# A fused attention and gMLP block: V's weight parts reordered, products moved into the first cycle, layer norm's factors moved into the spatial weights, ScalarE's side work limited

## The chip, the cores and the metric

The kernel runs on one core of one Trainium2 chip. A core has a matrix engine (TensorE, in the profile PE, with PEld for its weight loads), a vector engine (VectorE, DVE), an engine for activation functions (ScalarE, ACT), a general engine (GpSimd, POOL) and one that mostly issues DMAs (SyncE, SP). They run side by side, each working through its own list of instructions in order, and wait for each other by semaphores. Matmuls read SBUF and write PSUM.

The metric is the time of one execution on the device in microseconds (us), the median of several. Before the change it is 1957.76 us (1957.56 to 1959.02 in three runs).

## The reference

The input x (2048 x 512, all float32) is layer-normed to xn, and three things are added:

```python
x = A_x
xn = _layernorm(x, axis=-1)
return x + _A_ref(xn, A_wqkv, A_wo) + _B_ref(xn, B_w_in, B_w_sp, B_b_sp, B_w_out)
```

A is attention with 32 heads of 16 columns: qkv = xn @ wqkv, a softmax over 2048 keys of q k / 4, the sum over v, and a product with wo. B is a gated MLP over 1792 columns in two halves:

```python
z = _gelu(jnp.einsum("bsd,df->bsf", x, w_in))
z1 = z[..., :Fh]
z2 = _layernorm(z[..., Fh:], axis=-1)
g = jnp.einsum("ts,bsf->btf", w_sp, z2) + b_sp[None, :, None]
return jnp.einsum("bsf,fd->bsd", z1 * g, w_out)
```

Fh is 896. The spatial weights w_sp (2048 x 2048) mix the rows of z2, so a factor that belongs to row s of z2 may stand on column s of w_sp instead.

## The kernel before

**Products in two parts.** Dense products run in a reduced float32 form (F32R). To keep precision each operand is split into a high part, which is its rounded copy, and a low part, the operand less the high part; `mm3` (L169) adds three matmuls per 128-row block: low-free, low of the one, low of the other (L170, L171, L172 in the profile). What the text calls a product is one such triple over 512 (or 448) columns. A copy on ScalarE or a cast on POOL makes the high part, a subtraction on DVE or POOL the low one.

**Start.** Lines L836 to L906 load x and V's weights, normalise x (`norm_x`: statistics on DVE, the normalisation at L268 on ScalarE), transpose it on PE (`turn_x`), split it (`split`: copy L58 on ScalarE, subtraction L167 on DVE) and make V (`v_tile`) and the first Q and K. V's weights come in four row blocks wv0 to wv3. POOL casts all four (L857), DVE subtracts for blocks 0 to 2 and POOL for block 3 (`end` with `high`, L191).

**Attention.** From L995 a loop runs over half cycles (`half`). A cycle takes three tiles of scores (`scores`, tile st, L955), the exps of them on ScalarE (`exp`, tile pf, 128 x 1024), PV products (`pv`, tile o, L929), and, 27 tiles ahead, three tiles of scores in the other orientation (`max_mm`, tile mx, L650), whose maxima DVE takes (`max_red`, L658). An even half has two exps and one maximum, an odd half one and two. st and mx share three PSUM slots in turn. The halves below zero have mx only.

**Everything else is filler.** The dense products of Q and K (`qk_rest`), of the gMLP's halves (`z2_all`, `z1_all`), the spatial products (`spatial`), the output products (`mlp_out`, `attn_out`) stand in a queue of generators, and at the end of each odd half some are taken by a credit that spreads what is left over the tiles up to number 931. Before tile 0 each half may take four. Their evictions and what follows run on as generators in `side` (L1045): each is advanced once a half, if DVE's own account of the half (`load["D"]`) is under its limit. `bg` holds the loads and preparations of weights (`prepare`, `end`: on POOL a cast L196 and a subtraction L197).

**The planner's clock.** All of this is decided when the program is written out; the order of every engine's list is then fixed. A half counts 2.7 us (`HALF`); `gps(us)` adds a POOL operation's assumed time to POOL's own clock, and `pool_done` or `prepare` let later steps wait until that clock is reached. An `act` is booked as 0.16 + n/1400 us. Where a product's weights aren't ready by that clock, the queue pauses.

**z2.** `z2_norm` (L371) takes one 128-row tile of z2 through the gelu (POOL and one Tanh on ScalarE), the statistics (DVE, L393), the factors (small POOL operations, L396 to L404), the normalisation (Identity on ScalarE, L406), and the split into parts in two pieces of 512 and 384 columns (copy on ScalarE, subtraction on POOL, L412), which go to DRAM. z1's gelu (`z1_gelu`, L453) ends on DVE instead of POOL when POOL's clock is over 4 us behind.

Of the kernel before, what the change touches and what calls it, by code (L numbers as in the profile page):

```python
# [40 lines left out]
def fused_block(ctx, tc, x, wqkv, wo, w_in, w_spT, b_sp, w_out, out):  # L41
# [11 lines left out]

    load = {"A": 0.0, "D": 0.0}

    def act(out, in_, func, n, **kw):
        load["A"] += 0.16 + n / 1400.0
        return nc.scalar.activation(out, in_, func, **kw)  # L58

    def dve(n, rate=1):  # L60
# [12 lines left out]

    mrow = cp.tile([P, 32], F32R, name="mrow")
    nc.vector.memset(mrow.bitcast(F32), 0.0)


    qst = [cp.tile([P, S], F32R, name=f"qst{a}") for a in range(2)]
# [37 lines left out]
    def gps(us):  # L116
        pool[0] = max(pool[0], clock()) + us
        return nc.gpsimd
# [66 lines left out]
        move(dst, src)  # L185
        return t, rw, n

    def end(loaded, low=None, high=False):
        t, rw, n = loaded
        if high:  # L190
            low.tensor_sub(t[:, 1, :n], rw[:, :n], t[:, 0, :n].bitcast(F32))  # L191
        elif low:
            nc.scalar.activation(t[:, 0, :n], rw[:, :n], AF.Copy)
            low.tensor_sub(t[:, 1, :n], rw[:, :n], t[:, 0, :n].bitcast(F32))
        else:
            gps(0.6).tensor_copy(t[:, 0, :n], rw[:, :n])  # L196
            gps(1.3).tensor_sub(t[:, 1, :n], rw[:, :n], t[:, 0, :n].bitcast(F32))  # L197
        return t

    def prepare(out, loads, freed=None):  # L200


        loads, flight, made = list(loads), [], []
        while loads or flight or made:
            if made and clock() >= made[0][0]:
                _, k, t = made.pop(0)
                out[k] = t
            if flight and now[0] >= flight[0][0]:
                _, k, l = flight.pop(0)
                t = end(l)  # L210
                made.append((pool[0], k, t))
                rawfree.append(pool[0])
            if loads and len(rawfree) > 0 and clock() >= rawfree[0] and (freed is None or freed and now[0] >= freed[0]):
                rawfree.pop(0)
                if freed:
                    freed.pop(0)
                k, *a = loads.pop(0)
                flight.append((now[0] + 2, k, begin(*a)))
            yield
# [80 lines left out]

    def qk_group(m, g, w, tags=("d",)):
        for a in range(2):
            if now[0] < -2 and m:
                tags = ("d", "o")
            acc = dpsum(f"qk{m}_{a}_{g}", tags[a % len(tags)], ND)
            for c in range(ND):
                t = xnT[g, c]
                mm3(acc, w[a][:, 0, c * P:(c + 1) * P], w[a][:, 1, c * P:(c + 1) * P], t[:, 0, :], t[:, 1, :], c == 0, c == ND - 1)
                yield 650 + 0.5 * (c == ND - 1)
            if m == 0:  # L310
                run(qk_split(m, g, a, acc))
# [59 lines left out]
    def z2_norm(t, z):  # L371
# [27 lines left out]
        gps(0.3).tensor_mul(rs[:, 2:3], rs[:, 1:2], rs[:, 1:2])  # L399
        gps(0.3).tensor_mul(rs[:, 2:3], rs[:, 2:3], rs[:, 0:1])  # L400
        gps(0.3).tensor_scalar(rs[:, 2:3], rs[:, 2:3], -0.5, 1.5, ALU.mult, ALU.add)
        gps(0.3).tensor_mul(rs[:, 1:2], rs[:, 1:2], rs[:, 2:3])
        gps(0.3).tensor_mul(rs[:, 2:3], mv[:, 0:1], rs[:, 1:2])
        gps(0.3).tensor_scalar(rs[:, 2:3], rs[:, 2:3], -1.0, 0.0, ALU.mult, ALU.add)  # L404
        yield from pool_done()
        act(z, z, AF.Identity, FH, bias=rs[:, 2:3], scale=rs[:, 1:2])  # L406
        for j, (lo, w) in enumerate(((0, 512), (512, 384))):
            yield
            hl = hilo(f"z2hl{t}_{j}")
            act(hl[:, 0, :w], z[:, lo:lo + w], AF.Copy, w)  # L410
            yield
            gps(0.0025 * w).tensor_sub(hl[:, 1, :w], z[:, lo:lo + w], hl[:, 0, :w].bitcast(F32))  # L412
# [422 lines left out]
    with tc.manual_schedule(engines=engines):  # L835
# [17 lines left out]
        run(load_x(2))  # L853
        ones = big.tile([P, 512], F32, tag="raw", name="ones", bufs=3)
        nc.vector.memset(ones[0:32, 0:P], 1.0)
        for t, rw, n in wv:
            nc.gpsimd.tensor_copy(t[:, 0, :], rw)  # L857
        norm = norm_x(0, 2)
        next(norm)
        next(norm)  # L860
        wv = [end(l, (nc.vector, nc.gpsimd)[c == 3], True) for c, l in enumerate(wv)]
        turn_x(0, 0, 2)
        next(norm)
        nc.gpsimd.dma_start(cscr.rearrange("o (a b) -> (o a) b", b=P), ones[0:16, 0:P])
# [130 lines left out]
        for half in range(-2 * LEAD // 3, 2 * (N // 3 + 4)):  # L995
            b = 3 * (half // 2)
            ms = [b + LEAD] if half % 2 == 0 else [b + LEAD + 1, b + LEAD + 2]
            ns = [n for n in ([b, b + 1] if half % 2 == 0 else [b + 2]) if 0 <= n < N]
            now[0] = half
            flush()  # L1000
            for n in ns:
                if n == 16:
# [7 lines left out]
            tiles = [(scores, n) for n in ns]  # L1010
            for i, m in enumerate(ms):
                tiles.insert(1 if half % 2 == 0 else 2 * i, (max_mm, m))
            for make, n in tiles:
                make(n)
            while ended:
# [91 lines left out]
```

## Time and profile before

| what | us |
|---|---|
| median of three runs | 1957.76 |
| profiled execution | 1960.21 |
| its span, first to last instruction | 1958.4 |
| PE busy | 1938.7 |
| DVE busy | 1373.7 |
| ScalarE busy | 1232.5 |
| POOL busy | 725.5 |

The profile is of one execution. Its stages can be told by the tiles that PE writes: the start up to about 85 us, the halves without scores up to 140, then Q and K up to about 230, z2 to 455, z1 to about 675, the spatial products to about 1570, and the outputs. A row of the order of time gives start, duration, engine, line, operation, tiles and shape, and in brackets how long the engine was idle before it and what it waited for. Successive matmuls overlap, so a matmul's time in PE's list is the distance from one start to the next rather than its duration.

### The profile page before, as it was taken

The numbers are of one execution on the slowest core, as the hardware profiler recorded it, in microseconds if no ns is written. First come the engines' busy times: TensorE is split into PE (matmuls) and PEld (weight loads), VectorE is DVE, ScalarE is ACT, GpSimd is POOL, SyncE is SP. The second block draws the span as 40 slices with busy tenths as digits, with TensorE's granted clock in tenths as the row PEclk, the third lists the DMA queues.
The fourth block names the chain that finished last, engine by engine and source line by source line (L and its number), as shares of the span: only waits on it lengthen the run. The fifth ranks groups of instructions, "written<-read, shape, count | busy, mean of one in ns | idle before, by whom it ended". The sixth has DMA issues, their size and how long they took to land.

```text
span 1958.4 us, 32641 instructions
## 1 busy us (share of the span) xinstructions
PE 1938.7 (99%) x12559; PEld 1049.7 (54%) x12559; DVE 1373.7 (70%) x1565; ACT 1232.5 (63%) x1407; POOL 725.5 (37%) x790
## 2 busy tenths in 40 slices
PE   8999999999999999999999999999999999999998
PEld 7765555555555555555555555555555555555543
DVE  5356777777767677777777767777777777777872
ACT  4347778888677666656566656665666655556664
POOL 3334278889776931026122531017112400002100
PEclk9999999999999999999999999999999999999999
DMA  7566344363535535365545745346454645355323
GB/s 260 201 219 183 104 120 117 111 179 107 144 132 153 183 117 141 101 166 156 142 137 162 202 131 134 104 120 205 110 158 144 180 140 137 106 147 160 105 73 113
DMA packets 229202, 284.23 MB, mean 145 GB/s; under 512 B 35176, under 2 KB 134136, under 8 KB 226168
## 3 DMA queue, kind: packets, MB, share of 16 engines
q1 hardware_dynamic: 217240, 272.64, 47.9%
q0 software_dynamic: 2592, 8.46, 1.1%
q10 hardware_dynamic: 9216, 1.05, 0.4%
q8 instruction: 99, 1.62, 0.3%
q14 instruction: 55, 0.45, 0.1%
HBM read 188.51 MB, written 93.58 MB: 144 GB/s over the span
## 4 chain that ended last, share of the span: by engine, by line
PE 95%; DVE 2%; ACT 1%; issue 1%; DMA 0%; POOL 0%; SPq 0%; DVEq 0%; ACTq 0%
PE o L929 23%; PE mx L650 16%; PE st L955 15%; PE sp L170 7%; PE sp L172 5%; PE sp L171 5%; PE mo L170 2%; PE qk L170 2%; PE z1p L170 2%; PE z2p L170 2%; PE qk L171 1%; PE qk L172 1%; PE mo L171 1%; PE mo L172 1%; PE z1p L172 1%; PE z1p L171 1%
## 5 line engine op out<-in xcount | busy, mean ns | idle before, releaser
L658 DVE TENSOR_REDUCE mm<-mx 128x2 f32<-128x1024 f32 x1024 | 1221.9, 1222 | 498.2 <-PE mx L650 493.9
L58 ACT ACTIVATE pf<-st 128x1024 f32<-128x1024 f32 x1024 | 1028.8, 1025 | 620.0 <-PE st L955 591.6
L929 PE MATMUL o<-pf,vall 128*32 128x512 f32 (+1 forms) x5120 | 511.0, 513 | 0.0
L650 PE MATMUL mx<-kst,qst 48*128 48x512 f32 x2048 | 446.7, 434 | 2.7 <-ACT pf L58 1.8
L955 PE MATMUL st<-qst,kst 50*128 50x512 f32 x2048 | 445.2, 431 | 1.3 <-DVE mm L658 1.1
L650 PEld LDWEIGHTS mx<-kst,qst 48*128 48x128 f32 x2048 | 192.0, 185 | 268.4 <-ACT pf L58 169.6
L955 PEld LDWEIGHTS st<-qst,kst 50*128 50x128 f32 x2048 | 193.1, 185 | 164.0 <-issue 85.7
L929 PEld LDWEIGHTS o<-pf,vall 128*32 128x32 f32 x5120 | 131.4, 109 | 233.5 <-issue 211.5
L170 PE MATMUL sp<-wsp,zs 128*128 128x512 f32 x448 | 193.9, 433 | 0.3 <-DVE z1i L566 0.2
L573 POOL TENSOR_TENSOR z1i<-z1i,hhl 128x512 f32<-128x512 f32 x28 | 36.0, 1287 | 416.1 <-DVE z1i L566 413.3
L172 PE MATMUL sp<-wsp,zs 128*128 128x512 f32 x448 | 176.0, 393 | 0.0
L171 PE MATMUL sp<-wsp,zs 128*128 128x512 f32 x448 | 176.0, 393 | 0.0
L170 PEld LDWEIGHTS sp<-wsp,zs 128*128 128x128 f32 x448 | 83.9, 187 | 68.9 <-issue 51.8
L172 PEld LDWEIGHTS sp<-wsp,zs 128*128 128x128 f32 x448 | 84.1, 188 | 19.9 <-POOL wsp L197 0.5
L171 PEld LDWEIGHTS sp<-wsp,zs 128*128 128x128 f32 x448 | 84.4, 188 | 12.2
L196 POOL CAST wo<-wo0r 128x512 fp32r<-128x512 f32 x1 | 0.6, 612 | 189.6 <-DMA wo0r<-in_wo 189.6
L325 POOL TENSOR_TENSOR qkhl<-qr,qkhl 128x512 fp32r<-128x512 f32 x24 | 30.9, 1289 | 72.1 <-ACT qkhl L58 72.1
L170 PE MATMUL z2p<-w,xt 128*128 128x448 f32 x128 | 51.3, 401 | 0.0
L170 PE MATMUL mo<-wout,hp 128*128 128x512 f32 x112 | 48.5, 433 | 0.6 <-DVE xr L610 0.4
L711 POOL TENSOR_TENSOR ob<-ob 128x512 f32<-128x512 f32 (+1 forms) x16 | 20.6, 1287 | 72.8 <-DMA ob<-rscr 65.7
L172 PE MATMUL z2p<-w,xt 128*128 128x448 f32 x128 | 46.8, 366 | 0.0
L171 PE MATMUL z2p<-w,xt 128*128 128x448 f32 x128 | 46.7, 365 | 0.0
(382 smaller groups left out, 1986.3 us busy)
## 6 DMA issues: line engine op xcount, KB each, us to landing
zs<-z2scr SPq DMA_DIRECT2D x112, 512.0 KB
escr<-e SPq DMA_DIRECT2D x60, 256.0 KB
hscr<-hhl SPq DMA_DIRECT2D x28, 512.0 KB
xscr<-xnT POOLq DMA_DIRECT2D x16, 512.0 KB, 4.8
qscr<-qkhl SPq DMA_DIRECT2D x16, 512.0 KB
kscr<-qkhl SPq DMA_DIRECT2D x16, 512.0 KB
xt<-xscr SPq DMA_DIRECT2D x64, 128.0 KB
z2scr<-z2hl SPq DMA_DIRECT2D x32, 256.0 KB
```

The source lines that it names most:

```text
L58: return nc.scalar.activation(out, in_, func, **kw)
L170: nc.tensor.matmul(acc, lh, rh, start=first, stop=False)
L171: nc.tensor.matmul(acc, ll, rh, start=False, stop=False)
L172: nc.tensor.matmul(acc, lh, rl, start=False, stop=last)
L196: gps(0.6).tensor_copy(t[:, 0, :n], rw[:, :n])
L325: gps(1.3).tensor_sub(hl[:, 1 - a, :], src, hl[:, a, :].bitcast(F32))
L573: gps(1.3).tensor_add(z1, z1, hl[:, 1, :].bitcast(F32))
L650: nc.tensor.matmul(acc[:, j, :], qst[p % 2][rows, tt * P:(tt + 1) * P], kst[p % 2][rows, kc * 512:(kc + 1) * 512], start=True, stop=True)
L658: dve(1024).tensor_reduce(mmax[i // 16][:, :, t, kc], mstep.pop(i), AX.X, ALU.max)
L711: gps(1.3).tensor_mul(both[rows, 0, :], both[rows, 0, :], both[rows, 2, :])
L929: nc.tensor.matmul(acc[cols:cols + VW, a:a + w], vpack(kt - 1 + r, 2 * p + j), pf[:, j * 512 + a:j * 512 + a + w], start=(kt == 1 and a == ...
L955: nc.tensor.matmul(st[:, j, :], kst[p % 2][rows, kt * P:(kt + 1) * P], qst[p % 2][rows, c * 512:(c + 1) * 512], start=True, stop=True)
```

## The change

It has four parts. (1) V's weights: POOL casts blocks 0, 2 and 3 and ScalarE block 1, behind the normalisation of x's first tiles; DVE subtracts for blocks 0 and 1, POOL for 2 and 3. (2) The filler: halves 0 and 1 may take four products each, as the halves before; the PSUM tag of the Q and K products up to half 0 goes by whether the half is even ("o") or odd ("d"). (3) z2's layer norm: the Identity goes; ScalarE's copies subtract the mean as a bias, POOL subtracts the mean in place for the first piece before its subtraction, DVE makes the second piece's low part in one operation, and the factor 1/deviation of each row is kept in `zrs` and multiplied onto the raw spatial weights on POOL, one more operation for each of the 64 tiles. (4) `given` adds up the booked times of `act` in a half; when it is over 1.9 and fewer than three side generators are under way, none of them is advanced.

```diff
     def act(out, in_, func, n, **kw):
         load["A"] += 0.16 + n / 1400.0
+        given[0] += 0.16 + n / 1400.0
...
-    def end(loaded, low=None, high=False):
+    def end(loaded, low=None, high=False, scale=None):
         t, rw, n = loaded
+        if scale is not None:
+            gps(0.6).tensor_scalar(rw[:, :n], rw[:, :n], scale, 0.0, ALU.mult, ALU.add)
...
-                t = end(l)
+                t = end(l, scale=zrs[:, k[1]:k[1] + 1] if out is wsp else None)
...
-            if now[0] < -2 and m:
-                tags = ("d", "o")
+            if now[0] <= 0 and m:
+                tags = ("do"[now[0] % 2 == 0],)
...
-        gps(0.3).tensor_mul(rs[:, 1:2], rs[:, 1:2], rs[:, 2:3])
-        gps(0.3).tensor_mul(rs[:, 2:3], mv[:, 0:1], rs[:, 1:2])
-        gps(0.3).tensor_scalar(rs[:, 2:3], rs[:, 2:3], -1.0, 0.0, ALU.mult, ALU.add)
+        gps(0.3).tensor_mul(zrs[:, t:t + 1], rs[:, 1:2], rs[:, 2:3])
+        gps(0.3).tensor_scalar(rs[:, 2:3], mv[:, 0:1], -1.0, 0.0, ALU.mult, ALU.add)
         yield from pool_done()
-        act(z, z, AF.Identity, FH, bias=rs[:, 2:3], scale=rs[:, 1:2])
         for j, (lo, w) in enumerate(((0, 512), (512, 384))):
             yield
             hl = hilo(f"z2hl{t}_{j}")
-            act(hl[:, 0, :w], z[:, lo:lo + w], AF.Copy, w)
+            act(hl[:, 0, :w], z[:, lo:lo + w], AF.Identity, w, bias=rs[:, 2:3])
             yield
-            gps(0.0025 * w).tensor_sub(hl[:, 1, :w], z[:, lo:lo + w], hl[:, 0, :w].bitcast(F32))
+            if j:
+                dve(w).scalar_tensor_tensor(hl[:, 1, :w], z[:, lo:lo + w], rs[:, 2:3], hl[:, 0, :w].bitcast(F32), ALU.add, ALU.subtract)
+            else:
+                gps(0.0011 * w).tensor_scalar(z[:, lo:lo + w], z[:, lo:lo + w], rs[:, 2:3], 0.0, ALU.add, ALU.add)
+                gps(0.0025 * w).tensor_sub(hl[:, 1, :w], z[:, lo:lo + w], hl[:, 0, :w].bitcast(F32))
...
-        for t, rw, n in wv:
-            nc.gpsimd.tensor_copy(t[:, 0, :], rw)
         norm = norm_x(0, 2)
         next(norm)
         next(norm)
-        wv = [end(l, (nc.vector, nc.gpsimd)[c == 3], True) for c, l in enumerate(wv)]
+        for c in (0, 2, 3):
+            nc.gpsimd.tensor_copy(wv[c][0][:, 0, :], wv[c][1])
+        nc.scalar.activation(wv[1][0][:, 0, :], wv[1][1], AF.Copy)
+        wv = [end(l, (nc.vector, nc.gpsimd)[c > 1], True) for c, l in enumerate(wv)]
...
             now[0] = half
+            given[0] = 0.0
...
+            before = done
             for make, n in tiles:
...
-            side[:] = [g for g in side if load["D"] > limit or next(g, 0) is None]
+            side[:] = [g for g in side if load["D"] > limit or given[0] > 1.9 and len(side) < 3 or next(g, 0) is None]
             ready += len(ns)
-            if b < 0:
+            if b < 0 or b == 0 and done == before:
                 credit = 2600
```

More of the change, by code (lines that the diff above doesn't have):

```diff
@@ L54, in fused_block @@
     load = {"A": 0.0, "D": 0.0}
+    given = [0.0]
     def act(out, in_, func, n, **kw):
         load["A"] += 0.16 + n / 1400.0
+        given[0] += 0.16 + n / 1400.0
         return nc.scalar.activation(out, in_, func, **kw)
@@ L75, in fused_block @@
     nc.vector.memset(mrow.bitcast(F32), 0.0)
+    zrs = cp.tile([P, NT], F32, name="zrs")
     qst = [cp.tile([P, S], F32R, name=f"qst{a}") for a in range(2)]
```

## Prediction

> **What bounds the kernel now.** I read the page's busy times first, then busy time by stage, then the waits of PE, then the order of time at the places where PE idles.
>
> ```profile
> PE 1938.7 (99%) x12559; PEld 1049.7 (54%) x12559; DVE 1373.7 (70%) x1565; ACT 1232.5 (63%) x1407; POOL 725.5 (37%) x790
> ```
>
> ```profile
> core 0: us, PE busy (x) PEld busy (x) DVE busy (x) ACT busy (x) POOL busy (x), PEclk, DMA share, GB/s
> 0.00:50.00 50.00, 45.03 (x201) 36.07 (x202) 26.65 (x66) 24.70 (x46) 19.22 (x34) 0.97 0.74 263
> 140.00:150.00 10.00, 9.33 (x51) 4.72 (x51) 7.17 (x6) 7.36 (x9) 1.77 (x2) 1.00 0.48 152
> 230.00:455.00 225.00, 223.39 (x1496) 123.10 (x1494) 170.77 (x208) 180.17 (x222) 177.91 (x221) 1.00 0.46 125
> 690.00:1900.00 1210.00, 1208.20 (x7999) 632.28 (x7998) 887.29 (x972) 733.47 (x773) 277.62 (x268) 1.00 0.49 141
> ```
>
> PE bounds nearly everything: 1938.7 of 1958.4 us. The change removes no matmul, so it can only win back PE's idle or slowed time, and that is small: 4.97 us in the first 50 us, 0.67 in the first attention cycle (140 to 150), 1.61 in the z2 stage (230 to 455), 1.8 in the 1210 us from 690 on, and a tail that no part touches. So the question is whether a few microseconds come back, and whether a part takes some.
>
> **V's weight parts (start).** The chain is in order of time on all engines:
>
> ```profile
> 7.44 0.69 DVE L191 TENSOR_TENSOR qst<-wv0r,qst 128x512 fp32r<-128x512 f32 x1 [1.62 <-POOL qst L857]
> 7.51 1.09 POOL L857 CAST qst<-wv1r 128x512 fp32r<-128x512 f32 x1
> 8.55 0.61 POOL L857 CAST kst<-wv2r 128x512 fp32r<-128x512 f32 x1
> 8.64 1.07 DVE L191 TENSOR_TENSOR qst<-wv1r,qst 128x512 fp32r<-128x512 f32 x1 [0.51 <-POOL qst L857]
> 9.63 1.09 DVE L191 TENSOR_TENSOR kst<-wv2r,kst 128x512 fp32r<-128x512 f32 x1
> 10.64 1.40 DVE L167 TENSOR_TENSOR xnT<-xT,xnT 128x256 fp32r<-128x256 f32 x4
> 11.11 0.50 PE L171 MATMUL v<-qst,xnT 128*128 128x512 f32 x1 [1.65 <-DVE xnT L167]
> 12.11 0.63 PE L171 MATMUL v<-qst,xnT 128*128 128x512 f32 x1
> 12.53 0.63 PE L172 MATMUL v<-qst,xnT 128*128 128x512 f32 x1
> 14.16 1.28 POOL L197 TENSOR_TENSOR wqk<-wqk_0r,wqk 128x512 fp32r<-128x512 f32 x1
> 14.22 1.23 DVE L264 SCALAR_TENSOR_TENSOR rs<-mv,rs 128x2 f32<-128x2 f32 x1
> 15.49 1.52 ACT L268 ACTIVATE x<-x,rs 128x512 f32<-128x512 f32 x2 [1.50 <-DVE rs L264]
> 17.82 0.39 PE L172 MATMUL v<-kst,xnT 128*128 128x512 f32 x1
> 18.06 1.03 PE L276 MATMUL xT<-ident,x 128*128 128x128 f32 x8
> ```
>
> ```profile
> 8.20:11.60 3.40, 1.18 (x5) 0.64 (x4) 2.96 (x5) 1.32 (x4) 3.31 (x4) 1.00 1.11 355
> 11.70:15.00 3.30, 3.30 (x9) 2.62 (x8) 2.83 (x8) 0.29 (x1) 3.21 (x6) 0.50 1.06 388
> ```
>
> PE's second V product waits 1.65 us for xnT's low part, which stands on DVE behind three weight subtractions, though only the first is needed that early. Behind the gap the granted clock is 0.50 from 11.7 to 15.0: products start 0.42 us apart (12.11, 12.53) where later ones start 0.24 apart (17.82, 18.06).
>
> After the change DVE has two subtractions (c = 0, 1). The cast of c = 1 goes to ScalarE behind the normalisation of x; its data is there by 7.51, and an estimate of 0.6, as POOL's cast at 8.55, has it done near 8.1, before the copies of xnT need ScalarE. DVE's second subtraction (0.69) then ends near 8.85. xnT's first follows at once, and as PE now starts 0.47 us behind its start (10.64, 11.11), PE's second product comes near 9.3: 1.8 us earlier. POOL pays: cast 2 (its data there by 8.55) and cast 3 end near 9.45 and 10.05, then come two subtractions of 1.28 (14.16) instead of one, to 11.4 and 12.7. PE, at 0.24 a product, reaches the two products that need them near 11.0 and 12.2 and waits 0.4 and 0.5 us. If the clock stays full, the 24 products of two V tiles end near 15.7 instead of 18.06: -2.4 us. The x of the next transposes (15.49) follows DVE, which is free 1.8 us earlier, so it is there before 15. POOL's later work moves back by less than one subtraction; its next user, the first qk product, stands behind two more V tiles. Ends: 0 (POOL's parts take it all back) and -3.3 (1.8, and some eight of the nine products of the slow window at 0.18). I take -2.4.
>
> The Trainium skill, "TensorE: Matmul & The Clock Gate", Part 1, says that the clock is halved after an idle window of about 3.4 us and restored after a busy one. The trace has such a window, 3.4 us at half clock, behind one that was 1.18 us busy, so it need not be wholly idle. By that rule the window after the change, some 2.4 us busy, keeps the clock; if it did not, the term would be the first rival's.
>
> **Products in the first cycle.**
>
> ```profile
> 140.44 0.50 PE L955 MATMUL st<-qst,kst 50*128 50x512 f32 x2
> 140.77 0.40 PE L650 MATMUL mx<-kst,qst 48*128 48x512 f32 x2
> 141.01 0.40 PE L955 MATMUL st<-qst,kst 50*128 50x512 f32 x2
> 142.08 0.50 PE L650 MATMUL mx<-kst,qst 48*128 48x512 f32 x2 [0.67 <-ACT pf L58]
> ```
>
> Half 0 has no PV and no products: PE runs out of PSUM slots and idles 0.67 us for the first exp. The step from 141.01 to 142.08 is 1.07 where the same step takes 0.33 (140.44 to 140.77): 0.74 lost. Two shorter steps behind it add some 0.2. Four products (2.7 us) now stand at that place, from PSUM tag "o", which the first PV takes only two halves later; the copy out is queued behind one exp and done long before. Total products stay: those taken early are missing later. Gain 0.9 us; ends +0.3 (one more switch of matmul shape) and -1.2.
>
> **Layer norm's factors, z2 stage.**
>
> ```profile
> L58 ACT ACTIVATE z<-z,zrs 128x896 f32<-128x896 f32 x16 | 18.3, 1146 | 0.0
> L393 DVE BATCH_NORM_STATS2 zst<-z 128x6 f32<-128x448 f32 x32 | 18.3, 614 | 0.0
> L412 POOL TENSOR_TENSOR z2hl<-z,z2hl 128x384 fp32r<-128x384 f32 x16 | 16.2, 1011 | 0.0
> L363 POOL TENSOR_SCALAR z<-z 128x512 f32<-128x512 f32 x28 | 17.3, 619 | 2.5
> L364 POOL TENSOR_TENSOR z2u<-z2u,z 128x896 f32<-128x896 f32 x16 | 33.8, 2112 | 1.3
> ```
>
> ```profile
> PE mx L650 <- ACT pf L58: 1.2, 6, 0.2
> PE st L955 <- DVE mm L658: 0.4, 2, 0.2
> ```
>
> ```profile
> 429.44 1.12 ACT L58 ACTIVATE z<-z,zrs 128x896 f32<-128x896 f32 x1
> ```
>
> ```profile
> 428.85 0.50 PE L955 MATMUL st<-qst,kst 50*128 50x512 f32 x2
> 429.60 0.50 PE L650 MATMUL mx<-kst,qst 48*128 48x512 f32 x2 [0.25 <-ACT pf L58]
> ```
>
> The Identity over 896 columns goes (16 x 1.146 = 18.3 us of ScalarE); the copies that follow only gain a bias. In this stage ScalarE is 80% busy, and 1.2 of the 1.61 us that PE idles are exps that came late, the worst around such an Identity. A late exp costs more than its idle: the step to 429.60 is 0.75, 0.42 over the usual 0.33, for 0.25 of idle (1.7 times); the first cycle's was 0.74 for 0.67 (1.1 times). At 1.4 times, all of it is 1.7 us; I take -1.7. Ends 0 and -3.
>
> POOL in this stage (177.91 of 225 us): per tile a subtraction of 1.01 and one small op go, a tensor_scalar of 0.62 comes, about -0.6 x 16. PE never waits for it here: 0.
>
> DVE gains 16 subtractions of 384 columns. DVE's 512-column one takes 0.69 (7.44), so about 0.55 each. They read two SBUF tiles, and such an operation can wait for POOL, as 14.22 above against this:
>
> ```profile
> 23.88 0.16 DVE L264 SCALAR_TENSOR_TENSOR rs<-mv,rs 128x2 f32<-128x2 f32 x1
> ```
>
> The same 0.16 us operation lasted 1.23 beside a POOL subtraction. POOL is 79% busy with pieces of up to 2.11 us: a wait of some 0.7 on average, so 1.25 us of DVE each. The nearest thing now is the pair of statistics (2 x 0.61), 16 times, beside which all DVE waits together are 0.4 us of PE's idle. The same again, times 1.4, is +0.6; I take +0.7 for the longer tail. Ends 0 and +10 (0.65 us of PE for each of 16).
>
> The Trainium skill, "SBUF — State Buffer", Who interferes with whom, has this as a rule: a DVE instruction with two SBUF inputs and a GpSimd one that reads SBUF share a port pair under an exclusive lock, and the loser blocks for the whole instruction. The row agrees. It speaks against this part, and gives the third rival.
>
> **Factors on the spatial weights.** Each of 64 w_sp tiles gets one more tensor_scalar on POOL: 0.62 plus some 0.08 between operations. In the three later groups POOL is mostly idle (277.62 of 1210 us): 0, and if that cover were gone, as in the first. There 16 x 0.70 = 11.2 us come into a stretch where POOL works without a pause:
>
> ```profile
> 640.99 0.61 POOL L196 CAST wsp<-wsp_0r 128x512 fp32r<-128x512 f32 x1 [2.00 <-DMA wsp_0r<-in_w_spT]
> 699.83 1.29 POOL L197 TENSOR_TENSOR wsp<-wsp_15r,wsp 128x512 fp32r<-128x512 f32 x1
> ```
>
> ```profile
> 701.36 0.40 PE L170 MATMUL sp<-wsp,zs 128*128 128x512 f32 x1
> ```
>
> The last tile is ready at 701.12 and used at 701.36: no slack. The planner knows 0.6 of the 0.70, so it mostly holds products back, rather than let PE stand, and a cycle short of products is long on DVE anyway (three maxima). What it doesn't know, 16 x 0.1 = 1.6 us, can be PE idle. Its own rule (gelu's end on DVE when POOL is over 4 us behind) takes some back. Queued behind the weights on POOL are z1's gelus, whose users are a stage off. I take +0.5, ends 0 and +2.5.
>
> **ScalarE's limit.** Two exps count 1.78 in an even half, so any copy out reaches 1.9, and side chains wait unless three are under way. In the z2 stage three mostly are, so it seldom acts; in the spatial stage chains have slack. -0.2, ends -1 and +1.5 (z1 chains pile up and products pause).
>
> **Sum.** -2.4 - 0.9 - 1.7 + 0.7 + 0.5 - 0.2 = -4.0. The profiled execution took 1960.21 us (span 1958.4), so 1956.2 by it; it stands 2.45 over the median 1957.76, against which I forecast 1953.8, 0.20% less. A measurement here tells 0.2%, 3.9 us, from no change.
>
> **Rivals.** (1) The clock drops after all, or POOL's two subtractions eat the start: the start gives 0.8, the sum -2.4, 1955.4. For it: PE still has gaps of 0.5 before 12 us; against: the halving followed a far emptier window. (2) The limit and the missing Identity also remove late exps that show as no idle, in qk, z2 and z1: 3 us more, 1950.8. For it: ScalarE's 80%; against: PE's waits name little. (3) Slower: the port lock. If each of DVE's 16 subtractions costs PE 0.65 us, 10.4 replaces 0.7: +5.7, 1963.5. For it: the 1.23 row and POOL's 79%; against: 1.4 us of statistics cost little now. It decides from 0.55 us each (8.8 against 0.7 + 4.0 + 3.9 = 8.6).
>
> **How the numbers follow.** The sum 0.60, its own range 1951.5 to 1956, of which 0.37 lies beyond 0.2% and 0.23 within; rival 1 0.17 (within); rival 2 0.11 (faster); rival 3 0.12 (slower). Faster 0.48, within 0.40, slower 0.12. The range reaches to rival 2 with some of its spread and half way to rival 3: 1950 to 1960.
>
> **What will show it.** Start: xnT's low part near 8.9, PE's second V product before 9.6, granted clock 1.0 throughout, the second transposes near 15.7. First cycle: no idle of PE between 138 and 146. z2: PE's waits for exps below 0.5 us; DVE's new subtraction near 0.55, or over 1 us if the lock bites, and then PE waits for DVE's maxima. Spatial: the last tile of group 0 later, PE waits for wsp under 1.6 us. It is wrong if side chains pile up and products pause, which PE idle after 455 us would show.

## The result, and the profile after

The changed kernel takes 1974.32 us (median of 5 executions, 1971.65 to 1975.05), the kernel before 1957.72 beside it: ratio 1.0078 with the interval [1.0065, 1.0090]. It is 0.8% slower, 16.6 us, where 4.0 us less were forecast. The profiled execution took 1974.7 us (span 1972.9). Medians here and below are those of undisturbed executions, and each difference is to the kernel before as it ran beside that kernel.

Busy time of the page after:

```profile
PE 1945.3 (99%) x12559; PEld 1049.8 (53%) x12559; DVE 1386.5 (70%) x1584; ACT 1222.0 (62%) x1392; POOL 783.0 (40%) x830
```

Busy time by stage, after (stretch, then its length, PE, PEld, DVE, ACT and POOL with their instructions, granted clock, DMA share, GB/s):

```profile
0.00:50.00 50.00, 46.64 (x215) 37.60 (x216) 26.60 (x70) 25.78 (x48) 19.22 (x34) 1.00 0.79 283
140.00:150.00 10.00, 10.00 (x52) 5.97 (x50) 5.58 (x5) 7.37 (x11) 3.25 (x3) 1.00 0.88 307
230.00:455.00 225.00, 222.33 (x1488) 121.52 (x1487) 181.13 (x223) 171.13 (x209) 196.39 (x210) 1.00 0.46 123
640.00:710.00 70.00, 64.32 (x394) 32.07 (x390) 47.08 (x51) 39.81 (x47) 62.82 (x68) 0.98 0.56 164
```

The same stretch around the first spatial weights, before:

```profile
640.00:710.00 70.00, 69.97 (x452) 36.93 (x452) 48.17 (x51) 45.27 (x53) 60.94 (x64) 1.00 0.53 168
```

The start and the first cycle go the way that was forecast: 1.6 us less idle in the first 50 us, none between 140 and 150. The z2 stage idles 2.67 us where it idled 1.61. Its waits (in all, times, longest, in us):

```profile
PE st L965 <- DVE mm L667: 1.5, 5, 0.5
PE mx L659 <- ACT pf L61: 1.1, 1, 1.1
```

Those for exps are as before (1.1 for 1.2), where the forecast had looked for less than 0.5; those for DVE's maxima grew from 0.4 to 1.5. The largest hole is in the 70 us around the first spatial weights: 5.7 us of idle, a lower clock, 394 matmuls in place of 452 (all work stands some 4 us later there, so the two stretches don't hold quite the same). The forecast had 0.5 us there. PE's largest waits over the whole span, before:

```profile
PE mx L650 <- ACT pf L58: 1.8, 7, 0.7
PE st L955 <- DVE mm L658: 1.1, 4, 0.4
```

and after, without those of the start and the tail:

```profile
PE mx L659 <- ACT pf L61: 6.2, 9, 1.7
PE st L965 <- DVE mm L667: 3.0, 9, 0.5
PE sp L177 <- POOL wsp L204: 1.8, 3, 0.6
PE sp L175 <- POOL wsp L203: 1.5, 2, 0.8
```

One of the waits for exps, in order of time on all engines:

```profile
677.76 1.27 POOL L371 TENSOR_TENSOR z<-z 128x512 f32<-128x512 f32 x1
679.01 0.70 POOL L196 TENSOR_SCALAR wsp_7r<-wsp_7r,zrs 128x512 f32<-128x512 f32 x1
679.06 0.63 ACT L61 ACTIVATE z<-z 128x512 f32<-128x512 f32 x1 [3.84 <-DMA z1scr<-z]
679.60 2.93 ACT L61 ACTIVATE pf<-st 128x1024 f32<-128x1024 f32 x3
680.66 0.50 PE L659 MATMUL mx<-kst,qst 48*128 48x512 f32 x2 [1.73 <-ACT pf L61]
```

ScalarE stands idle for 3.84 us in front of a Tanh of z1 (z<-z), although exps are queued behind it. The wait is put down to a DMA, but POOL's last multiplication for that Tanh (677.76, 1.27) ends at 679.03, and the Tanh starts at 679.06. The three exps follow at once, and PE, whose score slots they free, has idled 1.73 us. The planner gives ScalarE the Tanh when its own sum of POOL's costs says that POOL is done; when POOL is later than that, the exps behind the Tanh are late too. So the waits for exps grew by 4.4 us, those for maxima by 1.9, and a third kind is new, 3.3 us for the weights themselves:

```profile
689.98 0.50 PE L175 MATMUL sp<-wsp,zs 128*128 128x512 f32 x1 [0.70 <-POOL wsp L203]
691.34 0.72 PE L177 MATMUL sp<-wsp,zs 128*128 128x512 f32 x1 [0.62 <-POOL wsp L204]
```

### The profile page after: what moved, and what is told of

The parts are those of the page before. It is cut to its first block, busy times and chain, and to the rows that moved or that the text cites. A ratio compares the mean times of both kernels' runs of the same rounds, so it can differ in the third digit from the quotient of the medians.

```text
span 1972.9 us, 32742 instructions
## 1 busy us (share of the span) xinstructions
PE 1945.3 (99%) x12559; PEld 1049.8 (53%) x12559; DVE 1386.5 (70%) x1584; ACT 1222.0 (62%) x1392; POOL 783.0 (40%) x830
## 4 chain that ended last, share of the span: by engine, by line
PE 90%; POOL 6%; DVE 3%; ACT 1%; issue 1%; DMA 0%; DVEq 0%; POOLq 0%; ACTq 0%
PE o L939 22%; PE mx L659 15%; PE st L965 15%; PE sp L175 7%; PE sp L177 5%; PE sp L176 5%; PE mo L175 2%; PE qk L175 2%; PE z2p L175 2%; PE qk L176 1%; PE qk L177 1%; DVE mm L667 1%; POOL wsp L204 1%; PE mo L177 1%; PE mo L176 1%; PE z1p L175 1%
## 5 line engine op out<-in xcount | busy, mean ns | idle before, releaser
L720 POOL TENSOR_TENSOR ob<-ob 128x512 f32<-128x512 f32 (+1 forms) x16 | 20.6, 1286 | 73.3 <-DMA ob<-rscr 65.1
```

Of the source, the lines that this page charges most:

```text
L720: gps(1.3).tensor_mul(both[rows, 0, :], both[rows, 0, :], both[rows, 2, :])
```

## The experiments

Below, "shift" says where time is lost: the start of the n-th pair of score products against the profile before, less 0.685 us (three matmuls 0.228 apart) for each further product that PE has done by then. Tile 24 lies near 182 us, 264 near 612 (ahead of the spatial weights), 336 near 740 (behind the first group of them), 984 near 1878. Each row is one profiled execution.

```
shift in us at tile        24     264     336     984
V's order alone          -3.3    -3.3    -3.6    -3.8
V + products             -4.0    -1.7    +3.4    +3.1
V + products, z1 costs   -3.8    -0.6    +0.7    +0.6
lead given back          -2.7    -2.4    -1.2    -1.3
scaling alone            -1.4    -1.4    +4.3    +7.5
layer norm's part alone  -2.0    +5.4   +10.0   +14.9
after without scaling    -3.7    +0.1    +4.3    +4.4
after without lead       -2.0    +1.9    +8.3   +12.8
after without limit      -3.6    +6.8   +17.4   +19.4
after, mean by mult, add -4.1    -1.5   +10.6   +15.3
after                    -3.9    +1.4   +10.7   +14.5
```

**The parts, taken apart.** First, V's order alone, then the change without the layer norm's part.

```diff
-        for t, rw, n in wv:
-            nc.gpsimd.tensor_copy(t[:, 0, :], rw)
...
-        wv = [end(l, (nc.vector, nc.gpsimd)[c == 3], True) for c, l in enumerate(wv)]
+        for c in (0, 2, 3):
+            nc.gpsimd.tensor_copy(wv[c][0][:, 0, :], wv[c][1])
+        nc.scalar.activation(wv[1][0][:, 0, :], wv[1][1], AF.Copy)
+        wv = [end(l, (nc.vector, nc.gpsimd)[c > 1], True) for c, l in enumerate(wv)]
```

> The kernel before with V's weight parts in the new order and nothing else. Theory A (each part acts in its own stage): the start is 2.7 to 3.0 us earlier, as in the profile after, and nothing later gives it back: 1954.8, -2.9 against before. Rival B (a head start only shifts when products are issued and is absorbed by the planner's budget later): 1957.5, no difference that can be told.

Measured: 1956.03 (-1.5), ratio 0.9993 [0.9983, 1.0002]. The median lies between the two theories and its interval reaches no change; the trace decides for A in that no later stage gives the gain back: the shift stays between -3.3 and -3.8. That the shift is larger than the median's gain is explained in the next section.

The second is the changed kernel with the layer norm's part undone, in the main these lines:

```diff
-            gps(0.6).tensor_scalar(rw[:, :n], rw[:, :n], scale, 0.0, ALU.mult, ALU.add)
...
+        act(z, z, AF.Identity, FH, bias=rs[:, 2:3], scale=rs[:, 1:2])
...
-            act(hl[:, 0, :w], z[:, lo:lo + w], AF.Identity, w, bias=rs[:, 2:3])
+            act(hl[:, 0, :w], z[:, lo:lo + w], AF.Copy, w)
```

> The changed kernel with the layer norm's part undone (V's order, first-cycle products and ScalarE's limit stay). Theory A (the layer norm's part is the whole loss): start -2.9 and first cycle -1.1 remain, the limit about 0: 1953.7, -4.0 against before. Rival C (the first cycle's products and the limit move products and side chains so that the later stages meet at a bad place): part of the loss stays, 1960 to 1966.

Measured: 1964.07 (+6.6), ratio 1.0035 [1.0025, 1.0044]. Theory A falls: even without the layer norm's part the rest loses 6.6 us. The third run is the complement: the layer norm's part changed, all else as before.

> The kernel before with the layer norm's part alone. Theory A: z2 stage +5.5, first spatial group +8, last spatial group +4: 1975, +17.5 against before, that is more than the whole change loses. Rival C: well below, 1964 to 1968.

Measured: 1975.14 (+17.6), ratio 1.0091 [1.0074, 1.0108]. So the layer norm's part alone loses more than the whole change does; +17.6 and +6.6 don't add to the +16.6 of both. The fourth leaves the 64 multiplications out:

```diff
         if scale is not None:
-            gps(0.6).tensor_scalar(rw[:, :n], rw[:, :n], scale, 0.0, ALU.mult, ALU.add)
+            pass
```

> The changed kernel without the 64 multiplications of the spatial weights (left out: layer norm's 1/deviation is then applied nowhere). Theory A: the z2 stage keeps its +5.5, the two spatial losses of 8.2 and 3.7 go: 1962.4, -12 against after. Rival D (the spatial stage's losses come from the POOL backlog and the products pushed back in the z2 stage, not from the 64 operations): 1970 to 1974.

Measured: 1963.77 (+6.3), ratio 1.0032 [1.0019, 1.0044]: the scaling costs 16.6 - 6.3 = 10.3 us in the changed kernel. Theory D falls. The two that follow split the remaining parts. V's order and the products, without the limit:

```diff
-            if now[0] < -2 and m:
-                tags = ("d", "o")
+            if now[0] <= 0 and m:
+                tags = ("do"[now[0] % 2 == 0],)
...
+            before = done
...
-            if b < 0:
+            if b < 0 or b == 0 and done == before:
```

> The kernel before with V's order and the first cycle's products, nothing else. Of the +6.9 that stayed when only the layer norm's part was undone, theory P (ScalarE's limit is the cause: side chains held back pile up behind it) says it goes: 1954.5, -3.0 against before. Theory Q (the 4 to 6 products taken early are the cause: later cycles stand a product short, with another maximum on DVE and exps in another order) says it stays: 1961 to 1964.

Measured: 1961.68 (+4.0), ratio 1.0021 [1.0012, 1.0031]. And V's order with the limit, without the products:

```diff
+        given[0] += 0.16 + n / 1400.0
...
+            given[0] = 0.0
...
-            side[:] = [g for g in side if load["D"] > limit or next(g, 0) is None]
+            side[:] = [g for g in side if load["D"] > limit or given[0] > 1.9 and len(side) < 3 or next(g, 0) is None]
```

> The kernel before with V's order and ScalarE's limit, nothing else. Theory P: 1962 to 1964, +5 or more against before. Theory Q: 1956, as V's order alone.

Measured: 1956.57 (-1.1), ratio 0.9996 [0.9986, 1.0006]. Theory Q holds and P falls: the four products of the first cycle, forecast at -0.9, cost +5.5 beside V's order. The limit's 0.4 can't be told from nothing: each interval here is some 2 us wide to either side.

**What the lead does.** The products gain their 1.2 us in the first cycle (shift -2.8 at tile 0, -4.0 at tile 24). From there on PE stands mostly 4 products ahead of where it was at the same tile before (up to 6 at times); the text calls this the lead. The gain is lost in two places: 2.3 us up to tile 264 and 5.1 us up to tile 336. The second place, V + products:

```profile
643.56 1.32 POOL L716 TENSOR_TENSOR ohl<-ob,ohl 128x512 fp32r<-128x512 f32 x1
650.65 1.28 POOL L364 TENSOR_TENSOR z<-z 128x512 f32<-128x512 f32 x1
651.96 0.63 ACT L58 ACTIVATE z<-z 128x512 f32<-128x512 f32 x1 [2.64 <-POOL z L364]
652.50 2.92 ACT L58 ACTIVATE pf<-st 128x1024 f32<-128x1024 f32 x3
653.56 0.50 PE L650 MATMUL mx<-kst,qst 48*128 48x512 f32 x2 [1.22 <-ACT pf L58]
```

Again a Tanh that waits for POOL, with exps behind it. Attention's own work on POOL stands elsewhere among the spatial weights. With V's order alone ohl ran at 634.12, when 279 tiles of scores had started, ahead of the first weight's cast (281); here it runs at 643.56, a cycle later (282), behind the first weight (280) and ahead of the second. If the lead is what hurts, giving the four products back at once must keep the 1.2 us and lose the rest.

```diff
+            if half == 5:
+                credit -= 2600
```

> V's order and the first cycle's products, with the planner's budget cut by 2.6 us in half cycle 5, so that the four products taken early are missing right behind and the lead is gone by score tile 36. Theory Q1 (the 3.5 to 4 products of lead that stood in the trace up to 700 us are what hurts: z1's gelus and the first spatial weights come a half cycle earlier against attention's own work on POOL, whose place is fixed by the cycles): the loss of 5.7 goes and the first cycle's 1.2 stay, 1955. Rival Q2 (the loss is tied to the products' PSUM tags or to the first cycle itself): 1960 to 1962.

Measured: 1959.10 (+0.9), ratio 1.0006 [0.9996, 1.0016]: 3.1 of the 5.5 us are gone (in the shift, 4.4 at tile 984), the 1.2 us don't stay (the missing products leave PE 0.86 us idle for a maximum at 154 us). Q1 is right in its main part, that the lead costs most of it; its number was a miss, and so was its reason in part, since ohl did move by a cycle. Next, the lead kept, and the planner told POOL's measured costs, here for the weights and the end of the gelu (each long operation of POOL likewise); and the same without the lead:

```diff
-            gps(0.6).tensor_copy(t[:, 0, :n], rw[:, :n])
-            gps(1.3).tensor_sub(t[:, 1, :n], rw[:, :n], t[:, 0, :n].bitcast(F32))
+            gps(0.69).tensor_copy(t[:, 0, :n], rw[:, :n])
+            gps(1.37).tensor_sub(t[:, 1, :n], rw[:, :n], t[:, 0, :n].bitcast(F32))
...
-        gps(0.0011 * n).tensor_scalar(u, u, 1.0, 1.0, ALU.mult, ALU.add)
-        gps(0.0024 * n).tensor_mul(x, x, u)
+        gps(0.27 + 0.00085 * n).tensor_scalar(u, u, 1.0, 1.0, ALU.mult, ALU.add)
+        gps(0.265 + 0.00215 * n).tensor_mul(x, x, u)
```

> V's order and the first cycle's products with the lead kept, and the planner's costs of POOL's long operations set to the durations and gaps of the trace (a gelu of z1 5.26 in place of 4.71 us, a weight pair 2.06 in place of 1.9). Theory F (the stalls come from Tanhs that the planner issues before POOL has their data): 1955 to 1957. Theory H (the lead leaves too little time for the weights whatever the planner knows): 1960 to 1963.

> V's order and the measured POOL costs, nothing else: the control to the run with the lead. Theory F: the plan has few late Tanhs to lose here (the profile before shows 1.2 us of waits for exps), 1955 to 1956. Theory H: 1956, and later products for want of z1's slots could make it 1958.

Measured: 1962.03 (+3.8), ratio 1.0019 [1.0009, 1.0028], with the lead; 1961.69 (+3.5), ratio 1.0015 [1.0005, 1.0025], without. Taken alone these would refute theory F. The trace shows another place: the qk weights now count as ready later, and ahead of the attention cycles PE has only maxima.

```profile
91.82 0.50 PE L650 MATMUL mx<-kst,qst 48*128 48x512 f32 x2 [0.88 <-DVE mm L658]
92.95 0.50 PE L650 MATMUL mx<-kst,qst 48*128 48x512 f32 x2 [0.63 <-DVE mm L658]
94.08 0.77 PE L650 MATMUL mx<-kst,qst 48*128 48x512 f32 x2 [0.63 <-DVE mm L658]
94.78 0.79 PE L170 MATMUL qk<-xnT,wqk 128*128 128x512 f32 x1
```

Before, products stood between these. 3 to 5 us are lost there, part of it because the clock halves behind it (granted 0.50 from 94.2 to 97.5 us; a matmul takes 0.63 to 0.79 where it takes 0.39 to 0.50 else). So the costs were corrected again for the gelus, z1's and z2's, which share the code, and for the spatial weights only:

```diff
-                t = end(l)
+                t = end(l, more=0.16 if out is wsp else 0.0)
```

> V's order and the first cycle's products with the lead; the planner's costs are corrected for the gelus and the spatial weights alone, so that the products before the attention cycles, whose loss at 92 to 96 us hid the result of the earlier run, stay where they were. PE's order is that of the run without corrected costs. Theory F (late Tanhs and weights issued by a wrong clock cost 5.1 us between 600 and 740): they go, 1956 to 1958. Theory H (the lead itself): 1961 to 1963.

Measured: 1960.02 (+1.6), ratio 1.0008 [0.9999, 1.0018]. PE's waits from 600 to 740 us, V + products:

```profile
PE mx L650 <- ACT pf L58: 1.4, 2, 1.2
PE sp L172 <- POOL wsp L197: 0.6, 1, 0.6
PE sp L170 <- POOL wsp L196: 0.5, 1, 0.5
```

and with the corrected costs:

```profile
PE st L956 <- DVE mm L658: 0.6, 2, 0.4
PE mx L650 <- ACT pf L58: 0.2, 1, 0.2
```

In this stretch theory F holds: the wait for exps falls from 1.4 to 0.2, that for weights goes, and the shift grows by 1.3 us in place of 5.1. The total is above what F expected, because 3.2 us are still lost between tiles 24 and 264 (2.3 without the corrected costs), where the gelus of z2 were booked anew too.

**What the two new POOL operations do.** The addition of the mean in the z2 stage, among the changed kernel's groups of instructions (busy us, mean ns of one, idle ahead of them):

```profile
L420 POOL TENSOR_SCALAR z<-z,zrs 128x512 f32<-128x512 f32 x16 | 32.2, 2013 | 3.9 <-ACT z2hl L61 3.4 <-DMA xt<-xscr 0.5
```

It was priced 0.62 from a multiplication and addition of two constants; two additions, one of a number for each partition, took 2.01. So they were written as the other pair:

```diff
-                gps(0.0011 * w).tensor_scalar(z[:, lo:lo + w], z[:, lo:lo + w], rs[:, 2:3], 0.0, ALU.add, ALU.add)
+                gps(0.0014 * w).tensor_scalar(z[:, lo:lo + w], z[:, lo:lo + w], 1.0, rs[:, 2:3], ALU.mult, ALU.add)
```

> The changed kernel with POOL's addition of the mean in the z2 stage as one multiplication by 1 and one addition in place of two additions (the same values). Theory A: the operation falls from 2.01 us to 0.70, POOL has 21 us less in the z2 stage and the exps are late less often: about -4, 1970. Rival E (POOL's time there isn't what delays the exps; the products, the limit or DVE's subtractions are): the operation falls all the same, the time stays at 1974.

Measured: the operation takes 0.72, the kernel 1974.28 (+16.6), ratio 1.0087 [1.0071, 1.0102].

```profile
L420 POOL TENSOR_SCALAR z<-z,zrs 128x512 f32<-128x512 f32 x16 | 11.5, 718 | 8.6 <-ACT z2hl L61 6.1 <-DMA kst<-kscr 2.5
```

Neither theory names what happened. The z2 stage gains what A says (shift -1.5 at tile 264 in place of +1.4), and the next stage loses it again: with other emission times one Tanh waits 4.89 us for POOL, and PE 3.46 us behind it.

```profile
653.20 1.26 POOL L371 TENSOR_TENSOR z<-z 128x512 f32<-128x512 f32 x1
654.49 0.63 ACT L61 ACTIVATE z<-z 128x512 f32<-128x512 f32 x1 [4.89 <-POOL z L371]
656.09 0.79 PE L659 MATMUL mx<-kst,qst 48*128 48x512 f32 x2 [3.46 <-ACT pf L61]
```

Then the planner was told the true costs of the two operations, which stayed as they were:

```diff
-                gps(0.0011 * w).tensor_scalar(z[:, lo:lo + w], z[:, lo:lo + w], rs[:, 2:3], 0.0, ALU.add, ALU.add)
+                gps(2.05).tensor_scalar(z[:, lo:lo + w], z[:, lo:lo + w], rs[:, 2:3], 0.0, ALU.add, ALU.add)
-            gps(0.6).tensor_scalar(rw[:, :n], rw[:, :n], scale, 0.0, ALU.mult, ALU.add)
+            gps(0.77).tensor_scalar(rw[:, :n], rw[:, :n], scale, 0.0, ALU.mult, ALU.add)
```

> The changed kernel with the planner told what POOL's two new operations take (2.05 in place of 0.563, 0.77 in place of 0.6); the operations are the same. Theory F (the planner's clock of POOL is wrong, so Tanhs are issued before their data is there and exps wait behind them): most of the 5 us of the z2 stage and several of the 12 us of the spatial stage go, 1963 to 1968. Theory G (POOL's work itself is too much, whatever is booked): 1972 to 1976.

Measured: 1968.45 (+10.8), ratio 1.0059 [1.0043, 1.0076]: 5.8 us of the loss go when the planner knows these two costs. Theory F missed its range by half a microsecond; G's lowest, 1972, is the end of the interval. That the 10.8 left have nothing to do with the planner's clock isn't shown by it, as POOL's other costs stayed booked short. All of POOL's long operations booked, with the cheap addition:

> The changed kernel with all of POOL's long operations booked as measured and the addition of the mean as multiply and add (0.79 booked). Theory F: below the 1968.5 of the run in which only the two new operations were booked, 1962 to 1966. Theory H (16 multiplications of 0.77 us are too much for POOL in the first group with the lead, whatever is booked): 1967 to 1972.

Measured: 1973.31 (+15.1), ratio 1.0079 [1.0063, 1.0095]. A miss for both: the loss at 92 us is in it again (its first score tile stands 0.9 us later than before's, where the changed kernel's stands 2.7 earlier), and a wait of 2.4 us at 657 us stayed. So this run doesn't tell what is left when every cost is right. And the scaling alone, on the kernel before, with factors of 1:

```diff
+    nc.vector.memset(zrs, 1.0)
...
+            gps(0.6).tensor_scalar(rw[:, :n], rw[:, :n], scale, 0.0, ALU.mult, ALU.add)
```

> The kernel before with the 64 multiplications of the spatial weights on POOL, by factors of 1 that a memset left (layer norm stays as it was, so the result is the same). Theory A (the 64 operations cost the same wherever the rest stands): +10.5, 1968. Theory J (without the lead and the late z2 stage the first group takes them with less): +5 to +9, most of it in the first group and the rest in the last two.

Measured: 1968.61 (+10.2), ratio 1.0052 [1.0036, 1.0069]. The number is theory A's: +10.2 alone, +10.3 beside everything else (the interval, 7 to 13.5 us, also takes in the upper part of J). As J had it, the first group loses most: 5.7 us of shift up to tile 336, then 3.2. Between 600 and 1400 us no exp is late here; PE waits for the weights themselves, 3.9 us, where before it has no such wait:

```profile
PE sp L175 <- POOL wsp L202: 2.7, 5, 0.6
PE sp L173 <- POOL wsp L201: 1.2, 3, 0.6
```

The later groups are not free. POOL in the stretch of the third group's weights, before and with the scaling alone:

```profile
1120.00:1180.00 60.00, 60.00 (x399) 31.94 (x399) 42.79 (x46) 35.50 (x38) 22.90 (x23) 1.00 0.44 138
```

```profile
1120.00:1180.00 60.00, 58.48 (x384) 30.34 (x383) 41.74 (x45) 34.96 (x37) 39.95 (x44) 1.00 0.53 153
```

POOL is busy 40 of 60 us and PE idles 1.5 us. An average over 1210 us says nothing on such a stretch, in which a group's weights come one behind the other.

**Could the work go to DVE?** The scaling folded into the two parts of the weights, the low part on DVE; and the same place for the low part, without scaling, in V + products:

```diff
+                if out is wsp:
+                    gps(0.77).tensor_scalar(l[0][:, 0, :l[2]], l[1][:, :l[2]], zrs[:, k[1]:k[1] + 1], 0.0, ALU.mult, ALU.add)
+                    made.append((pool[0], k, l))
...
+                if out is wsp:
+                    t, rw, n = t
+                    dve(n).scalar_tensor_tensor(t[:, 1, :n], rw[:, :n], zrs[:, k[1]:k[1] + 1], t[:, 0, :n].bitcast(F32), ALU.mult, ALU.subtract)
```

> The changed kernel with the scaling folded into the spatial weights' two parts: POOL writes the high part as weight times factor (0.77 with its gap), DVE the low part (weight times factor minus high part, in one operation). POOL does 1 operation for each tile in place of 3, 0.77 us in place of 2.83. Theory K (POOL's work in the groups' stretches is the cause of the spatial losses): the 8.2 and 3.7 us and the lead's 5 us go, 1958 to 1962. Rival L (64 more operations of 0.7 to 0.9 us on DVE, most beside POOL, make the maxima late): 1966 to 1972.

> V's order and the first cycle's products with the lead, and the spatial weights' low part on DVE in place of POOL (0.69 each on DVE, 1.37 less on POOL). Theory K: the 5.1 us between 600 and 740 go, what the lead costs in the z2 stage (2.0) stays: 1956 to 1957.5. Rival L: DVE's maxima come late, 1960 to 1964.

Measured: 1973.71 (+15.3), ratio 1.0077 [1.0062, 1.0092], and 1975.75 (+17.4), ratio 1.0090 [1.0075, 1.0105]. Both lie above rival L's ranges too, but its mechanism is there: PE's waits for DVE's maxima are 9.2 us in the first (3.0 in the changed kernel) and 11.7 in the second (2.9 in V + products). In the second:

```profile
1115.59 0.61 POOL L220 CAST wsp<-wsp_2r 128x512 fp32r<-128x512 f32 x1 [6.07 <-DMA wsp_2r<-in_w_spT]
1116.23 1.12 DVE L212 TENSOR_TENSOR wsp<-wsp_2r,wsp 128x512 fp32r<-128x512 f32 x1 [3.90 <-POOL wsp L220]
1118.54 0.80 PE L969 MATMUL st<-qst,kst 50*128 50x512 f32 x2 [3.72 <-DVE mm L671]
```

POOL stood idle for 6.07 us until the weight had landed, DVE 3.90 for the cast, and the maxima behind it on DVE held PE for 3.72. The load itself was issued late, at 1110.10, when 543 tiles of scores had started (540 in V + products): the edit also frees the raw weight's place later, as DVE's operation now ends its use. It is the same pattern with DVE in ScalarE's place: an engine that PE waits for stands still in front of work that depends on POOL. That POOL's load is the cause (theory K) is neither shown nor refuted by these two.

**The limit.** The z2 side costs 17.6 - 10.2 = +7.4 alone, but 6.3 - 6.6 = -0.3 beside the limit and the lead. Two runs of the change, each without one of them:

> The changed kernel with ScalarE's limit undone. Theory M (the limit is what saves the z2 stage: without it ScalarE gets Tanhs early and exps wait): 1979 to 1982, +5 to +7 against after. Theory N (the lead saves it, or all losses end in one stretch and are paid once): 1972 to 1976; the limit's own +1.4 to +2.8 would even make it 1972.

> The changed kernel with the first cycle's products undone. Theory M: the z2 side costs nothing here either, 1956.0 + 1.4 for the limit + 10.2 for the scaling: 1967.6. Theory N: as the layer norm's part alone with V's order and the limit, 1974 to 1976.

Measured: 1978.67 (+20.6), ratio 1.0112 [1.0094, 1.0130], and 1970.85 (+12.7), ratio 1.0065 [1.0049, 1.0081]. Without the limit the time is at theory M's lower end; without the lead it is 3 us above M's 1967.6 and below N's range. PE's waits from 230 to 530 us without the limit:

```profile
PE st L962 <- DVE mm L664: 5.2, 9, 2.3
PE mx L656 <- ACT pf L58: 2.6, 5, 1.2
```

and in the changed kernel:

```profile
PE mx L659 <- ACT pf L61: 2.5, 3, 1.2
PE st L965 <- DVE mm L667: 2.3, 7, 0.5
```

The limit takes 2.9 us off the waits for DVE's maxima, which the forecast had looked for under ScalarE. It is worth 20.6 - 16.6 = 4.0 us here. Where the layer norm's part is not there it saves nothing: +0.4 beside V's order and +2.6 beside V's order and the lead, both within the noise of two intervals.

## Why the prediction was wrong

Adding the parts in one order, measured: V's order -1.5, the products +5.5, the layer norm's part +16.6 (10.2 of it the scaling, so 6.4 the z2 side), the limit -4.0: together +16.6. Forecast: -2.4, -0.9, +0.5 and -1.0, -0.2: -4.0.

- **V's weight parts, -2.4: mechanism right, size off, -1.5.** xnT's low part starts at 9.13 (forecast 8.9), PE's second product at 9.61 (before 9.6), the second transposes at 15.02 (15.7), the clock is 1.00 throughout. What was mis-sized is the state of before. Its half-clock window from 11.7 to 15 belongs to that one execution: the run with the scaling alone starts with the same program but for one small memset and shows

```profile
0.00:50.00 50.00, 45.68 (x208) 36.77 (x209) 27.87 (x69) 24.57 (x46) 18.76 (x34) 1.00 0.77 273
```

  so 1.00 where the profile before has 0.97, and its first score tile comes 1.4 us earlier. The wait of 1.65 us that the term took off is 0.82 there: wv0 had landed for POOL's first cast at 5.79, at 6.80 in the profile before. The second transposes end at 17.3 in that run and at 15.8 with V's order alone: 1.5 us, the size of the measured gain. The prediction noted that the profiled execution stood 2.45 us over the median, and still took its window off the median. (A slip on the way: cast 2, from 8.55 and 0.61 long, would end near 9.2, not 9.45; it changes nothing here, as no product waited for POOL's parts.)
- **First cycle, -0.9: right there (-1.2), wrong as a term.** "Total products stay: those taken early are missing later" counted them and stopped. The step that failed is that work taken early changes nothing but its own place: it changed the order of z1's gelus, the first weights and attention's work on POOL, in the stretch that the prediction itself had quoted as one without a pause (641 to 701 us). Measured +5.5; 3.1 go when the lead is given back.
- **z2, Identity -1.7 and POOL "-0.6 x 16: 0".** The Identity is gone and ScalarE has 9 us less to do in the stage (171.13 for 180.17), yet PE's waits for exps there are 1.1 us for 1.2, and 2.5 for 1.2 up to 530 us, where the last tiles of z2 end. The step that failed is that less work on ScalarE makes the exps come in time: what counts is what stands in front of them. The one that is late in the stage (PE idle 1.11 at 435.88) stands behind two Tanhs in a row (432.50, 1.93 together), the next (1.17 at 484.48) behind a Tanh that waited 1.99 us for POOL. POOL's new operation took 2.01 in place of 0.62: the nearest row had another pair of operations. "PE never waits for it" overlooked that ScalarE does, in order, through the planner's clock. The net of the z2 side, forecast -1.0, was +6.4 without the limit and about 0 with limit and lead.
- **DVE's subtractions, 1.25 each: an upper bound that held.**

```profile
L418 DVE SCALAR_TENSOR_TENSOR z2hl<-z,zrs,z2hl 128x384 fp32r<-128x384 f32 x16 | 13.7, 857 | 0.0
```

  0.86 us on average. Rival 3 had the side and a part of the mechanism (waits for DVE's maxima of 1.5 us in place of 0.4 in the stage, and without the limit 5.2 up to 530 us), but these subtractions were not moved by themselves, so what they cost stays open.
- **Scaling, +0.5: the largest error, measured 10.2.** Its duration was right (0.70). Three steps failed. "The planner mostly holds products back, rather than let PE stand": PE stood, 3.9 us for weights with the scaling alone. It can hold back only for costs that it knows, and it was short on POOL's other work too (a weight pair 1.9 for 2.06, a gelu of z1 4.71 for 5.26); that this is why it failed is argued, not shown by a run of its own. "The three later groups: 0", from an average over 1210 us: 3.2 us of shift. And no loss of clock was counted (below; with the scaling alone it is granted 0.50 from 699.6 to 702.9 us). The upper end of 2.5 held little more than the 1.6 us that the planner did not know of the scaling.
- **Limit, -0.2:** +0.4 as the range had it, -4.0 beside the rest, which the text had no case for.

Of its signs of being wrong the last one showed, PE idle after 455 us, but not for the reason given with it: side chains that the limit holds back are theory P, which fell.

Open: what in the z2 side makes the 3 us that are left beside the limit when the lead is gone (the change without the lead against theory M), and how the 10.2 us of the scaling split between waits and the clock. The profiled execution of the scaling alone stands 2.2 us under its median and the one of before 2.45 over, so the two traces show 6.1 of them. What DVE's subtractions cost, and what would be left of the loss with every cost of POOL booked right and the early loss at 92 us avoided, no run shows.

## What to carry to other kernels

Where an order is written by a planner with a cost table, price each new operation from a row with the same pair of operations and the same operand kinds, book it, and then ask what the shifted order does at the place with the least slack, because here that place decided and not the place of the edit. An operation on an engine that PE never waits for still costs when an in-order engine that PE does wait for is handed work that depends on it; look for idle in front of that engine's dependent instruction. Before taking a stall off a median, see whether another execution of the same code shows it.

## What the runs showed of the hardware

POOL's tensor_scalar on 128x512 f32 took 2013 ns as two additions, one of them with an operand for each partition, and 718 ns as a multiplication and an addition, one of them with such an operand, same tile, same place (the changed kernel and the run that swaps the pair).

The clock halved three times in the changed kernel ahead of its tail, at 486.6, 691.4 and 1384.3 us. The stretches of 3.4 us ahead of the last two, the halved ones behind them, and one that was emptier and kept the clock:

```profile
687.98:691.40 3.42, 2.10 (x8) 0.94 (x8) 1.89 (x2) 0.85 (x1) 3.27 (x5) 1.00 0.80 258
691.40:694.80 3.40, 3.40 (x19) 1.58 (x23) 1.23 (x1) 1.09 (x2) 3.25 (x4) 0.51 0.38 111
1380.90:1384.30 3.40, 1.97 (x9) 0.88 (x10) 0.47 (x1) 0.00 (x0) 2.33 (x3) 1.00 0.10 37
1384.30:1387.70 3.40, 3.40 (x22) 0.72 (x18) 2.48 (x7) 1.63 (x2) 0.33 (x1) 0.51 0.69 230
677.70:681.10 3.40, 1.67 (x20) 0.53 (x12) 1.52 (x2) 2.04 (x3) 3.19 (x4) 1.00 0.97 340
```

PE was busy 2.10 and 1.97 us ahead of the halvings, with 8 and 9 instructions, and 1.67 with 20 where the clock stayed. So two waits of 0.6 to 0.8 us for a weight cost, by an estimate, another 1.7 us of matmul time behind them (3.4 us at half clock), and the three halvings some 5 us in all; busy time in these rows does not tell where the border lies. The Trainium skill, "TensorE: Matmul & The Clock Gate", Part 1, gives the half clock "after ≥1 idle window (~3.4µs)", of windows that run freely, 3413 ns long. The two halvings lie 692.9 us, 203.0 such windows, apart, which agrees, but a window that is 60% busy by these rows was enough.
